# A fused attention and mixer block: x loads split and re-ordered around the query weights, two transposes moved from TensorE to DMA, a 384/128 last store, new instruction sequences

## The chip, the cores and the metric

One NeuronCore of a Trainium2 chip runs the whole program in one launch. The metric is device time in microseconds (us); lower is better. Five engines run their own instruction streams: TensorE (PE, matrix products into PSUM), VectorE (DVE), ScalarE (ACT), GpSimd (POOL) and SyncE (SP, here only a queue that issues DMAs). They wait for each other on semaphores alone.

## What is computed

x is 2048 tokens by 512 features, bfloat16. A pre-norm linear-attention block with 32 heads is followed by a pre-norm gMLP block whose spatial mixing multiplies a 2048 by 2048 matrix.

```python
def _A_ref(x, wqkv, wo):                       # x is layernorm(x)
    qkv = ...(x @ wqkv)...
    phi = lambda t: jnp.where(t > 0, t + 1, jnp.exp(t)) + 1e-06
    pq, pk = (phi(q), phi(k))
    kv = jnp.einsum('bhsd,bhse->bhde', pk, v)
    z = jnp.einsum('bhsd->bhd', pk)
    num = jnp.einsum('bhqd,bhde->bhqe', pq, kv)
    den = jnp.einsum('bhqd,bhd->bhq', pq, z)[..., None] + 1e-06
    return (num / den)... @ wo
def _B_ref(x, w_in, w_sp, b_sp, w_out):        # x is layernorm(h)
    z = _gelu(jnp.einsum('bsd,df->bsf', x, w_in))
    z1 = z[..., :Fh].copy()
    z2 = _layernorm(z[..., Fh:], axis=-1)
    g = jnp.einsum('ts,bsf->btf', w_sp, z2) + b_sp[None, :, None]
    return jnp.einsum('bsf,fd->bsd', z1 * g, w_out)
h = x + _A_ref(_layernorm(x, axis=-1), A_wqkv, A_wo)
return h + _B_ref(_layernorm(h, axis=-1), B_w_in, B_w_sp, B_b_sp, B_w_out)
```

## The kernel before

The 2048 tokens are 16 tiles of 128 (tile 0 to 15), in four groups of four. All weights and activations stay in SBUF.

**How order is made.** The program lists every operation once, with what it reads and writes. Two written-out tables then fix the execution: `ORDER` is a permutation of all operations, from which each engine takes its own in turn, and `SLOT` gives every PSUM or scratch tile its place. `schedule()` reads both, adds a wait wherever an operation needs what another engine wrote, or a PSUM bank that another still holds, and `run()` issues the waits and the instructions. The costs written into the operations play no part in execution. Each engine is strictly in order, so an instruction that waits holds all behind it. SP issues in this order: the loads of x and of the key and query weights, the DMA transposes of normalised x, 16 DMA transposes of the mixing matrix, those of the second block's input, the other 48 of the mixing matrix, the stores. POOL issues the loads of the value weights (wv), `w_in`, `wo`, the bias and `w_out`; wv waits for the last DMA transpose of normalised x, and `w_in` and `wo` stand behind it.

**The first stage**, where most of the change lies. For each tile n:

- DVE takes mean and variance (`stats`, L568, and the aggregate, L572). 1/sqrt is made on ACT for tiles 0 to 3 (Ln L582, Exp L584), and on POOL for the pairs from (4, 5) on (two steps, L587 and L589). DVE normalises (L603).
- The normalised tile is transposed. For tiles in `X_BY_PE` PE does it in four products of 128 columns (L633, "TR n" below), and ACT copies the result from PSUM (L640). For the others SP issues a DMA transpose (L625), which needs neither PE nor ACT.
- PE makes the keys of the tile, four products of 512 columns (L715, "K n"). For each pair of tiles ACT takes the exponential (L692) and for odd pairs the relu (L694), and DVE joins them to the feature map phi (L695, then L698 or, on even pairs, L701).
- PE multiplies the normalised tile with phi of the keys, summing over all tiles (L747, "XK n.0" and "XK n.1", two products each).
- For each group PE makes the queries of its four tiles in four blocks of 128 features (L729, "Q g f", four products each), which needs all four transposes of the group; phi on them runs as for keys.

Before the first transposes PE has nothing to multiply. It runs products of constants (L556, `keep_busy`, "idle products"): eight at once, three that wait for the first statistics, one that waits for the first Exp, and later two short ones of 256 columns after each of TR 0 and TR 1.

**The rest.** The sums over the keys (L759), den/spread steps (L829, L844), attention output (L879), second layernorm, the two halves of the first gMLP product (L911, L942), the spatial mixing (L981, 448 products), and the output product (L999), whose result DVE adds to h (L1005) and SP stores (L1007). The last tile's output is made in two passes of 256 columns.

Of the kernel before, what the change touches and what calls it, by code (L numbers as in the profile page):

```python
# [10 lines left out]
P = 128  # L11
# [1 line left out]


ORDER = [
# [36 lines left out]
]  # L52
SLOT = [
# [6 lines left out]
]  # L60


# [292 lines left out]
def bass_sequential_preLN__linear_attn_block__mixer_gmlp__prompt_kernel(  # L355
# [20 lines left out]
    WARM = 8  # L376
    EPS_PHI, EPS_DEN, EPS_LN = 1e-6, 1e-6, 1e-5
    CG = 32
    X_BY_PE, H_BY_PE = (0, 1, 2, 3, 4, 5), ()
    Q_RELU = (True, True, True, True)  # L380
    K_RELU = (1, 3, 5, 7)
    CENTRED = ()
    A_STATS = ()
    R_POOL = (4, 6, 8, 10, 12, 14)
    COPY_DVE = ()
    LN1 = [[0], [1], [2], [3], [4, 5], [6, 7], [8, 9], [10, 11], [12, 13], [14, 15]]
    N2_ACT = range(16)
    VIA_ACT = ((0, 0), (1, 0), (2, 0), (3, 0))
# [37 lines left out]
    def small(shape, dtype):  # L426
        n = (int(np.prod(shape)) * mybir.dt.size(dtype) + GRAIN - 1) // GRAIN * GRAIN
        o = at[0]
        at[0] += n
        return View(s_sm, o, shape, dtype)  # L430
# [60 lines left out]
    def load(eng, name, dst, src, nbytes, bias=0.0, behind=(), cost=0.5):  # L491
        o = op(eng, cost, lambda e: e.dma_start(dst.ap(), src), w=[dst], dma=(name, False), nbytes=nbytes,  # L492
               bias=bias, land=2.3)
        for p in behind:
            o.deps[p] = True
        return o
# [3 lines left out]
    BIG = 1000.0  # L500

    def load_x(eng, a, b, bias=BIG, **kw):
        more = {2: 103e3, 4: 70e3}.get(a, 0)
        xl[a] = load(eng, f"x{a}", x[a:b, :], x_dram[a * P:b * P, :].rearrange("(n p) d -> p n d", p=P),
                     int((b - a) * P * D * 2 + more), bias, **kw)

    load_x("sp", 0, 1)
    load_x("sp", 1, 2)
    load_x("sp", 2, 4)
    load("sp", "wk", wqkv[:, D:2 * D], w3[:, :, D:2 * D], D * D * 2 + 50000)  # L510
    for a in (4, 6):
        load_x("sp", a, a + 2)
    for a in (8, 10):
        load_x("sp", a, a + 2)
    load_x("sp", 12, 16)
    load("sp", "wq", wqkv[:, 0:D], w3[:, :, 0:D], D * D * 2)
    for a, b in zip(g.ops, g.ops[1:]):
        b.after.append(a)

# [89 lines left out]
    def normalise_act(dst, src, rs, nm, n=512):  # L609
        op("act", act_c(n, 2) + 0.04, lambda e: e.activation(dst.ap(), src.ap(), ACT.Identity, bias=nm.ap(), scale=rs.ap()),  # L610
           r=[src, rs, nm], w=[dst])

    def minus(m, rs, nm):
        op("pool", 0.25, lambda e: e.tensor_scalar(nm.ap(), m.ap(), -1.0, None, op0=ALU.mult), r=[m], w=[nm])
        op("pool", 0.25, lambda e: e.tensor_tensor(nm.ap(), nm.ap(), rs.ap(), ALU.mult), r=[nm, rs], w=[nm])
# [31 lines left out]
    for grp in LN1:  # L647
# [21 lines left out]
        rs_op[grp[0]] = g.ops[-1]  # L669
        for i, n in enumerate(grp):  # L670
            d = xn1[n, :]
            normalise(d, x[n, :], Row(st_x, n), 6, rs[i:i + 1], negative=n in A_STATS)
            transposed(n, lambda d=d: d, xT, n in X_BY_PE)

    for gate, n, cost, count in ((first[0], 512, 2 * MM, 3), (rs_op[0], 512, 2 * MM, 1), (tr_op[0], 256, MM, 2),
                                 (tr_op[1], 256, MM / 2, 2)):
        for i in range(count):
            keep_busy(n, cost, [], [gate] if gate.eng != "pe" else [])
            if gate.eng == "pe":
                g.ops[-1].after.append(gate)  # L680
# [335 lines left out]
                for n in range((tg - 1) * TPG, tg * TPG):  # L1016
                    project(n, [(0, D)])
    for n in range((NG - 1) * TPG, NT):
        project(n, [(0, D)] if n < NT - 1 else [(0, D // 2), (D // 2, D)])


    g.schedule()
# [55 lines left out]
```

## Time and profile before

| | us |
|---|---|
| median of 3 runs (243.77 to 244.08) | 244.07 |
| the profiled execution's own time | 243.96 |
| its span, first to last instruction | 242.2 |

The profile is of that one execution. "Busy" is time in which an engine has an instruction in flight. Products on PE overlap, so a row of several products is read by the distance from its start to the next row's start. A row of the timeline gives its start, its length, engine and line, the operation, its output and input, how many instructions it merges, and, in brackets, idle time before it and what ended that. SPq and POOLq are the queues on which DMAs are issued; the time "to landing" runs from the issue to the completion.

### The profile page before, as it was taken

What the parts mean: (1) busy time and instruction counts of PE and PEld (TensorE: products, weight loads), DVE (VectorE), ACT (ScalarE), POOL (GpSimd) and SP (SyncE); (2) the same over time, 40 slices, a digit from 0 to 9 for tenths busy, and PEclk for the clock granted to TensorE, in tenths of its full rate; (3) what the DMA queues carried; (4) which work ended last, traced back from release to release, by engine and by line L of the source; (5) the groups of instructions that cost most, each with busy time, mean ns of one, the idle gap of its engine ahead of it and who ended that gap; (6) DMA issues with size and microseconds to landing.
All of it is one profiled execution on the core that took longest, in us unless ns stands there. A gap on an engine that the chain in (4) does not pass through costs nothing.

```text
span 242.2 us, 3026 instructions
## 1 busy us (share of the span) xinstructions
PE 238.3 (98%) x1175; PEld 108.8 (45%) x1175; DVE 135.2 (56%) x269; ACT 85.1 (35%) x107; POOL 34.1 (14%) x87
## 2 busy tenths in 40 slices
PE   8999999999999999999999999999999999999995
PEld 3544443433444444445444444444444444444443
DVE  4999654589999967656533223251332513322443
ACT  3875744898588598564500010000000000000000
POOL 5316021002316542122100000000000000000000
DMA  6920459954324231459344444446200100000022
GB/s 199 321 43 18 94 106 337 232 122 96 46 43 128 47 46 22 87 119 231 88 108 92 107 86 95 100 108 94 83 0 0 65 24 0 0 0 3 0 87 87
DMA packets 55598, 21.57 MB, mean 89 GB/s; under 512 B 49472, under 2 KB 54720, under 8 KB 55584
## 3 DMA queue, kind: packets, MB, share of 16 engines
q1 hardware_dynamic: 54640, 17.05, 32.7%
q0 software_dynamic: 944, 4.33, 5.5%
q8 instruction: 9, 0.15, 0.3%
q14 instruction: 5, 0.04, 0.1%
HBM read 7.47 MB, written 2.10 MB: 40 GB/s over the span
## 4 chain that ended last, share of the span: by engine, by line
PE 91%; DVE 4%; DMA 2%; ACT 2%; SPq 1%; issue 0%
PE ps L981 40%; PE ps L942 10%; PE ps L911 10%; PE ps L999 10%; PE ps L747 6%; PE ps L879 5%; PE ps L715 5%; PE ps L729 4%; DMA xh<-in_A_x_dram 2%; DVE small L568 1%; SPq L492 1%; DVE xT_pq_z L698 1%; DVE xh L884 0%; DVE xT_pq_z L859 0%; DVE e L695 0%; PE ps L844 0%
## 5 line engine op out<-in xcount | busy, mean ns | idle before, releaser
L981 PE MATMUL ps<-wsp,pk_xn_z 128*128 128x512 bf16 x336 | 73.8, 379 | 0.0
L988 DVE TENSOR_TENSOR e<-ps,e 128x512 bf16<-128x512 f32 x28 | 19.4, 691 | 66.0 <-PE ps L981 66.0
L981 PEld LDWEIGHTS ps<-wsp,pk_xn_z 128*128 128x128 bf16 x336 | 32.8, 98 | 39.5
L942 PE MATMUL ps<-hT,win 128*128 128x512 bf16 x112 | 26.6, 379 | 0.0
L911 PE MATMUL ps<-win,hT 128*128 128x512 bf16 (+1 forms) x128 | 26.0, 353 | 0.0
L999 PE MATMUL ps<-wout,xT_pq_z 128*128 128x512 bf16 (+1 forms) x119 | 24.7, 367 | 0.0
L981 PE MATMUL ps<-wqkv_wsp,pk_xn_z 128*128 128x512 bf16 x112 | 24.3, 379 | 0.0
L947 ACT ACTIVATE xT_pq_z<-ps 128x1024 bf16<-128x1024 f32 (+1 forms) x16 | 14.4, 913 | 23.9 <-PE ps L942 23.9
L568 DVE BATCH_NORM_STATS2 small<-xh 128x6 f32<-128x512 bf16 x32 | 20.7, 678 | 3.3 <-DMA xh<-in_A_x_dram 3.3
L920 DVE BATCH_NORM_STATS2 small<-pk_xn_z 128x6 f32<-128x512 bf16 (+1 forms) x32 | 18.3, 611 | 7.2 <-ACT pk_xn_z L916 7.1
L692 ACT ACTIVATE e<-ps 128x1024 bf16<-128x1024 f32 x16 | 16.5, 1029 | 9.7 <-PE ps L715 6.1
L911 PEld LDWEIGHTS ps<-win,hT 128*128 128x128 bf16 x128 | 12.5, 98 | 12.7 <-ACT e L854 0.3
L916 ACT ACTIVATE pk_xn_z<-ps 128x896 bf16<-128x896 f32 x16 | 14.5, 914 | 8.9 <-PE ps L911 8.8
L1005 DVE TENSOR_TENSOR e<-ps,xh 128x512 bf16<-128x512 f32 (+1 forms) x17 | 11.2, 660 | 11.3 <-PE ps L999 11.3
L999 PEld LDWEIGHTS ps<-wout,xT_pq_z 128*128 128x128 bf16 x119 | 11.6, 98 | 12.8
L981 PEld LDWEIGHTS ps<-wqkv_wsp,pk_xn_z 128*128 128x128 bf16 x112 | 11.0, 98 | 13.2
L942 PEld LDWEIGHTS ps<-hT,win 128*128 128x128 bf16 x112 | 10.9, 98 | 12.6 <-ACT pk_xn_z L916 0.4
L589 POOL TENSOR_TENSOR small<-small 128x2 f32<-128x2 f32 x22 | 16.0, 727 | 1.2
L587 POOL TENSOR_SCALAR small<-small 128x2 f32<-128x2 f32 x22 | 6.4, 297 | 67.6 <-DVE small L572 67.4
L747 PE MATMUL ps<-pk_xn_z 128*128 128x512 bf16 x64 | 15.6, 379 | 0.0
L729 PE MATMUL ps<-xT_pq_z,wqkv_wsp 128*128 128x512 bf16 x64 | 15.5, 380 | 0.0
L715 PE MATMUL ps<-wqkv_wsp,xT_pq_z 128*128 128x512 bf16 x64 | 15.3, 379 | 0.0
(72 smaller groups left out, 191.0 us busy)
## 6 DMA issues: line engine op xcount, KB each, us to landing
out_dram<-e SPq DMA_DIRECT2D x15, 128.0 KB, 1.7
win<-in_B_w_in_dram POOLq DMA_DIRECT2D x1, 1792.0 KB, 9.2
xh<-in_A_x_dram SPq DMA_DIRECT2D x5, 256.0 KB, 4.7
wqkv_wsp<-in_A_wqkv_dram SPq DMA_DIRECT2D x2, 512.0 KB, 5.7
wout<-in_B_w_out_dram POOLq DMA_DIRECT2D x1, 896.0 KB, 6.4
wsp<-in_B_w_sp_dram SPq DMA_TRANSPOSE x48, 2.9
xh<-in_A_x_dram SPq DMA_DIRECT2D x1, 512.0 KB, 6.2
wqkv_wsp<-in_A_wqkv_dram POOLq DMA_DIRECT2D x1, 512.0 KB, 4.8
```

What stands on the lines that cost most here:

```text
L568: op("dve", dve_c(512), lambda e: e.bn_stats(s6.ap(), src.ap()), r=[src], w=[s6])
L589: return op("pool", 0.7, lambda e: e.tensor_tensor(dst.ap(), dst.ap(), h.ap(), ALU.pow), r=[dst, h], w=[dst])
L692: op("act", act_c(n), lambda e: e.activation(lo.ap(), t(flat).ap(), ACT.Exp), r=[t()], w=[lo])
L715: i = e.matmul(t(bank(ti)).ap(), lhsT=lhs.ap()[:, c, :], rhs=rhs.ap()[:, c, :], start=(c == 0), stop=(c == KD - 1))
L729: r_ = e.matmul(t(bank(i)).ap(), lhsT=lhs.ap()[:, c, :], rhs=rhs.ap()[:, c, :], start=(c == 0), stop=(c == KD - 1))
L747: r = e.matmul(txk[h](bank(i)).ap(), lhsT=xx.ap()[:, c * P:(c + 1) * P], rhs=kk.ap(), start=(n == 0), stop=(n == NT - 1))
L911: k = e.matmul(t(bank(i)).ap()[:, 0:b - a], lhsT=l.ap()[:, c, :], rhs=win[c, a:b].ap(), start=(c == 0), stop=(c == KD - 1))
L920: op("dve", dve_c(b - a), lambda e, s6=s6, src=src: e.bn_stats(s6.ap(), src.ap()), r=[src], w=[s6])
L942: k = e.matmul(t(bank(i)).ap(), lhsT=l.ap()[:, c, :], rhs=r_.ap()[:, c, :], start=(c == 0), stop=(c == KD - 1))
L981: k = e.matmul(t(bank(0)).ap(), lhsT=l.ap()[:, s - a, :], rhs=r_.ap()[:, s - a, :], start=(s == 0), stop=(s == NT - 1))
L988: op("dve", dve_c(512), lambda e: e.tensor_tensor(gb().ap(), t(bank(0)).ap(), bsp().ap()[:, tg * GW:(tg + 1) * GW], ALU.add), r=[t(), bsp( ...
L999: k = e.matmul(t(bank(0)).ap()[:, 0:b - a], lhsT=l.ap()[:, fc, :], rhs=wout[fc, a:b].ap(), start=(fc == 0), stop=(fc == KF - 1))
```

## The change

Parts:

1. The x load of tiles 2 and 3 together becomes two loads, of tile 2 ahead of the key weights and of tile 3 behind them. The load of the query weights moves from the end of SP's list to ahead of the load of tiles 4 and 5.
2. Tiles 4 and 5 are no longer transposed by PE but by DMA: eight products and two ACT copies are gone, two DMA transposes are added at the head of SP's ten.
3. Of the three idle products that wait for the first statistics one is dropped.
4. The last tile's output is made in passes of 384 and 128 columns in place of 256 and 256.
5. `ORDER` and `SLOT` are new throughout (nearly every number differs; their lines are left out below).

Two helpers that nothing uses are added as well (`normalise_pool`, and lists `N1_POOL`, `N1_ACT` that are empty). The byte figures in `load_x` (`more`) enter the planned costs alone.

```diff
-    X_BY_PE, H_BY_PE = (0, 1, 2, 3, 4, 5), ()
+    X_BY_PE, H_BY_PE = (0, 1, 2, 3), ()
...
+    N1_POOL = ()
+    N1_ACT = ()
...
     load_x("sp", 0, 1)
     load_x("sp", 1, 2)
-    load_x("sp", 2, 4)
+    load_x("sp", 2, 3)
     load("sp", "wk", wqkv[:, D:2 * D], w3[:, :, D:2 * D], D * D * 2 + 50000)
+    load_x("sp", 3, 4)
+    load("sp", "wq", wqkv[:, 0:D], w3[:, :, 0:D], D * D * 2)
     for a in (4, 6):
         load_x("sp", a, a + 2)
     for a in (8, 10):
         load_x("sp", a, a + 2)
     load_x("sp", 12, 16)
-    load("sp", "wq", wqkv[:, 0:D], w3[:, :, 0:D], D * D * 2)
...
-    for gate, n, cost, count in ((first[0], 512, 2 * MM, 3), (rs_op[0], 512, 2 * MM, 1), (tr_op[0], 256, MM, 2),
+    for gate, n, cost, count in ((first[0], 512, 2 * MM, 2), (rs_op[0], 512, 2 * MM, 1), (tr_op[0], 256, MM, 2),
                                  (tr_op[1], 256, MM / 2, 2)):
...
-        project(n, [(0, D)] if n < NT - 1 else [(0, D // 2), (D // 2, D)])
+        project(n, [(0, D)] if n < NT - 1 else [(0, D - P), (D - P, D)])
```

Read out of the two `ORDER` tables, the instructions of PE from the end of the first idle products on, up to XK 8.0:

```
before: TR 0, idle, idle, TR 1, idle, idle, K 0, TR 2, K 1, K 2, TR 3, TR 4, TR 5, K 3, K 4, Q g0 f0, Q g0 f1,
  K 5, XK 0.0, 0.1, 1.1, 1.0, Q g0 f2, Q g0 f3, XK 2.0, 3.0, 2.1, 3.1, K 6, K 7, XK 4.1, 5.1, Q g1 f2, Q g1 f3,
  XK 4.0, 5.0, Q g1 f0, Q g1 f1, XK 6.0, K 8, K 9, XK 6.1, K 10, XK 7.1, K 11, XK 7.0, XK 8.0
after:  TR 0, idle, TR 1, idle, TR 2, idle, idle, K 0, K 2, TR 3, K 1, Q g0 f2, K 3, Q g0 f0, Q g0 f3, Q g0 f1,
  XK 0.1, 1.1, 0.0, 1.0, K 4, K 5, XK 2.0, 3.0, 2.1, 3.1, K 6, K 7, XK 4.0, Q g1 f0, Q g1 f1, XK 5.0, K 8,
  XK 4.1, K 9, Q g1 f2, Q g1 f3, XK 5.1, 6.1, 7.1, 6.0, 7.0, XK 8.0
```

and those of DVE in the new order, from the first tile to the phi of keys 8 and 9 ("join" is L701 or L698):

```
stats 0, 1, aggr 0, 1, stats 2, aggr 2, norm 0, 1, 2, stats 3, aggr 3, norm 3, stats 4, 5, aggr 4, 5, stats 7, 6,
min k0, norm 4, aggr 7, norm 5, join k0, aggr 6, stats 8, min k1, stats 9, norm 6, join k1, norm 7, stats 11,
aggr 9, 8, stats 10, min q0.0, stats 14, norm 8, min k2, aggr 14, join k2, aggr 10, norm 9, min q0.2, aggr 11,
stats 12, 15, join q0.2, aggr 15, norm 10, min k3, aggr 12, norm 11, stats 13, norm 15, aggr 13, join q0.0,
min q1.0, join k3, join q1.0, min k4, norm 12, join k4
```

ACT begins with Ln and Exp of tiles 0, 1 and 2 in both orders; then it copied TR 0 and TR 1 and took Ln 3, Exp 3, copy 2 and the first exponential (of keys 0 and 1), and now it copies TR 0, 1 and 2, takes Ln 3 and Exp 3, copies TR 3, and goes on to that exponential. POOL's order for the pairs is (4, 5), (6, 7), (8, 9), (10, 11), (14, 15), (12, 13), and that of SP's transposes follows the tiles' numbers. Behind the sums over the keys, PE ran two den steps, Q g3 f0, the product with the value weights (L796), a spread step, Q g3 f1 and then the product with wo (L814); now two more blocks of queries and a second spread step stand ahead of L814: den, den, Q g2 f2, L796, spread, Q g2 f3, Q g2 f0, spread, Q g2 f1, L814.

More of the change, by code (lines that the diff above doesn't have):

```diff
@@ L502, in load_x @@
     def load_x(eng, a, b, bias=BIG, **kw):
-        more = {2: 103e3, 4: 70e3}.get(a, 0)
+        more = {2: 40e3, 3: 60e3, 4: 70e3}.get(a, 0)
         xl[a] = load(eng, f"x{a}", x[a:b, :], x_dram[a * P:b * P, :].rearrange("(n p) d -> p n d", p=P),
@@ L611, in normalise_act, with normalise_pool @@
            r=[src, rs, nm], w=[dst])
+    def normalise_pool(dst, src, m, rs):
+        op("pool", 0.9, lambda e: e.tensor_scalar(dst.ap(), src.ap(), m.ap(), rs.ap(), op0=ALU.subtract,
+                                                  op1=ALU.mult), r=[src, m, rs], w=[dst])
     def minus(m, rs, nm):
@@ L671, in bass_sequential_preLN__linear_attn_block__mixer_gmlp__prompt_kernel @@
             d = xn1[n, :]
-            normalise(d, x[n, :], Row(st_x, n), 6, rs[i:i + 1], negative=n in A_STATS)
+            if n in N1_POOL:
+                normalise_pool(d, x[n, :], st_x[n, 6:7], rs[i:i + 1])
+            elif n in N1_ACT:
+                nm = small([1], FP32)
+                minus(st_x[n, 6:7], rs[i:i + 1], nm.all())
+                normalise_act(d, x[n, :], rs[i:i + 1], nm.all())
+            else:
+                normalise(d, x[n, :], Row(st_x, n), 6, rs[i:i + 1], negative=n in A_STATS)
             transposed(n, lambda d=d: d, xT, n in X_BY_PE)
-    for gate, n, cost, count in ((first[0], 512, 2 * MM, 3), (rs_op[0], 512, 2 * MM, 1), (tr_op[0], 256, MM, 2),
+    for gate, n, cost, count in ((first[0], 512, 2 * MM, 2), (rs_op[0], 512, 2 * MM, 1), (tr_op[0], 256, MM, 2),
                                  (tr_op[1], 256, MM / 2, 2)):
```

84 rows, old and new, of tables (ORDER, SLOT) are left out of this document.

## The prediction

> **What bounds the kernel now.** I read the chain of waits first, then busy time by stretches, then the timelines of the first 12 us.
>
> ```profile
> PE 91%; DVE 4%; DMA 2%; ACT 2%; SPq 1%; issue 0%
> ```
> ```profile
> 0.00:6.00 6.00, 5.17 (x14) 1.78 (x15) 2.85 (x9) 2.22 (x6) 3.60 (x22) 1.00 0.67 197
> 6.00:11.00 5.00, 4.59 (x39) 2.52 (x38) 4.83 (x16) 3.96 (x9) 1.00 (x2) 1.00 1.09 354
> 12.00:24.00 12.00, 12.00 (x57) 5.49 (x56) 12.00 (x30) 8.27 (x10) 4.95 (x9) 1.00 0.13 27
> 48.00:80.00 32.00, 31.85 (x162) 13.87 (x161) 31.28 (x54) 25.79 (x33) 8.40 (x21) 1.00 0.40 86
> 80.00:230.00 150.00, 150.00 (x708) 69.10 (x707) 65.31 (x133) 28.89 (x34) 12.67 (x29) 1.00 0.30 64
> ```
>
> The columns are the stretch, its length, and busy time of PE, PEld, DVE, ACT and POOL; the granted clock, DMA share and GB/s end the row. PE is the bound from 12 us to the tail, with no hole worth the name. So time can be won in two ways: fewer products, or real products that begin earlier. DVE is just as full from 12 to 24 and nearly so from 48 to 80; it is second in line. What PE does at the start:
>
> ```profile
> 0.83 5.25 PE L556 MATMUL ps<-const-bfloat16-1.0 128*128 128x512 bf16 x12 [0.83 <-PEq L1063]
> 5.91 0.40 PE L633 MATMUL ps<-small,pk_xn_z 128*128 128x128 bf16 x4
> ...
> 7.00 1.04 PE L715 MATMUL ps<-wqkv_wsp,xT_pq_z 128*128 128x512 bf16 x4
> 7.87 0.39 PE L633 MATMUL ps<-small,pk_xn_z 128*128 128x128 bf16 x4
> 8.09 1.89 PE L715 MATMUL ps<-wqkv_wsp,xT_pq_z 128*128 128x512 bf16 x8
> 9.82 0.39 PE L633 MATMUL ps<-small,pk_xn_z 128*128 128x128 bf16 x4
> 10.59 0.72 PE L633 MATMUL ps<-small,pk_xn_z 128*128 128x128 bf16 x8 [0.38 <-DVE pk_xn_z L603]
> 11.14 1.89 PE L715 MATMUL ps<-wqkv_wsp,xT_pq_z 128*128 128x512 bf16 x8
> ```
>
> From row to row, a transposed tile costs 0.22 (7.87 to 8.09), a key block K 0.865 (8.09 to 9.82 is two). TR 3 begins at 9.82 and TR 4 only at 10.59: PE stands 0.55 there and waits for the normalised tile 4. K 3 begins at 11.14, and from there PE never stops until the sums over the keys. Why tile 4 is late:
>
> ```profile
> 2.68 4.51 DMA xh<-in_A_x_dram
> ```
>
> In the chain, the load of tiles 4 and 5 takes from 2.68 to 7.19, and PE reaches for them as soon as DVE has them.
>
> **The change, part by part.** I compare the moment when PE begins K 3 with the whole remainder (K 3 to K 15, all Q, all XK) before it. Before, that is 11.14, with all transposes done.
>
> DVE, ACT and POOL of the same stretch:
>
> ```profile
> 2.98 1.29 DVE L568 BATCH_NORM_STATS2 small<-xh 128x6 f32<-128x512 bf16 x2 [2.98 <-DMA xh<-in_A_x_dram]
> ...
> 5.26 0.40 DVE L603 TENSOR_SCALAR pk_xn_z<-xh,small 128x512 bf16<-128x512 bf16 x1
> ```
> ```profile
> 4.83 0.33 ACT L584 ACTIVATE small<-small 128x1 f32<-128x1 f32 x2
> 5.78 0.29 ACT L582 ACTIVATE small<-small 128x1 f32<-128x1 f32 x1 [0.62 <-DVE small L572]
> 6.11 0.20 ACT L584 ACTIVATE small<-small 128x1 f32<-128x1 f32 x1
> 6.34 1.08 ACT L640 ACTIVATE xT_pq_z<-ps 128x512 bf16<-128x512 bf16 x2
> ```
> ```profile
> 8.81 0.29 POOL L587 TENSOR_SCALAR small<-small 128x2 f32<-128x2 f32 x1 [4.57 <-DVE small L572]
> 9.19 0.71 POOL L589 TENSOR_TENSOR small<-small 128x2 f32<-128x2 f32 x1
> ```
>
> *x tile 2 alone, one idle product less.* Exp of tile 0 is done near 5.02 (4.83 and half of the pair), but its normalise starts at 5.26, behind the statistics of tile 2, which had to wait for 256 KB. With 128 KB I put them before 4.5, so norm 0 runs 5.1 to 5.5 and norm 1 to 5.8. Ln and Exp of tile 2 begin at 5.2 in place of 5.78 and end near 5.75; norm 2 ends at 6.2. PE's eleven products end one (5.08/12 = 0.42) earlier than 5.91, at 5.48: TR 0 at 5.65, TR 1 at 5.95, TR 2 at 6.3. ACT's first copy no longer waits for Exp 2 (its end at 6.31 is where the copies began): it starts 0.2 after TR 0, near 6.05, and ends at 6.65. K 0 begins at 6.7, with three transposes done where before it was 7.00 with two. If tile 2 does not land sooner than the pair did, K 0 stays at 7.0: those are the two ends, 0 and 0.3; I take 0.3, as the row of the load of two tiles leaves no reason for a half load to take as long.
>
> *K 0 to K 3.* Copies follow each other at 0.5: copy 2 ends at 7.65, so K 2, now ahead of K 1, waits 0.13 and runs 7.7 to 8.56. Tile 3 lands behind the key weights; its Ln waits for ACT until 7.55, Exp ends at 8.05, norm 3 at 8.5, so TR 3 fits at 8.57, then K 1 from 8.8 to 9.65. K 3 follows, one query block having been drawn ahead of it. PE thus has the same remainder before it at 9.65, against 11.14: **1.49 earlier**. By parts: 0.3 (start), 0.22 (TR 2 already in), 0.45 (TR 4, TR 5 gone), 0.6 (their wait gone, with its restart), less 0.13 and some hundredths.
>
> *Tiles 4 and 5 by DMA, query weights first.* The 512 KB put ahead of them take 1.48 at the 354 GB/s of the row from 6 to 11: landing at 8.67 in place of 7.19. Statistics 8.7 to 9.95, aggregates to 10.2, POOL's two steps 1.1 (8.81 to 9.90) to 11.4, norm 4 ends at 12.05, norm 5 at 12.45.
>
> ```profile
> xT_pq_z<-pk_xn_z SPq DMA_TRANSPOSE x10, 2.5
> ```
> ```profile
> 22.62 10.35 SPq L625 DMA_TRANSPOSE xT_pq_z<-pk_xn_z  x8
> ```
>
> A DMA transpose lands after 2.5 and holds SP 1.3 (10.35/8): tile 4 at 14.6, tile 5 at 15.9. PE wants K 4 after five blocks and four half blocks from 9.65, at 15.7, and K 5 at 16.55. Covered by 1.1 and 0.65; without that cover each 0.1 of lateness is 0.1 of time.
>
> *The new order up to K 15.* All later tiles now come from a DVE that starts their statistics at 8.7. Its costs:
>
> ```profile
> L568 DVE BATCH_NORM_STATS2 small<-xh 128x6 f32<-128x512 bf16 x11 | 7.2, 679 | 0.0
> L603 DVE TENSOR_SCALAR pk_xn_z<-xh,small 128x512 bf16<-128x512 bf16 x13 | 5.0, 402 | 0.0
> L695 DVE TENSOR_SCALAR e<-e 128x1024 bf16<-128x1024 bf16 x9 | 3.7, 416 | 2.2 <-ACT e L694 2.1
> L698 DVE TENSOR_TENSOR xT_pq_z<-e 128x1024 bf16<-128x1024 bf16 x4 | 2.8, 689 | 0.1
> L701 DVE SCALAR_TENSOR_TENSOR pk_xn_z<-ps,e 128x1024 bf16<-128x1024 f32 x2 | 2.4, 1207 | 0.0
> L572 DVE BATCH_NORM_AGGREGATE small<-small 128x2 f32<-128x6 f32 x12 | 1.9, 171 | 0.0
> ```
>
> Each overlaps the next by 0.08 (the pair at 2.98 takes 1.29, not 1.38), so the steps are 0.60, 0.32, 0.34, 0.61, 1.13 and 0.09. From stats 4 to the join of keys 4 and 5 there are 9, 5, 4, 1, 2 and 7 of them: 11.9, done at 20.7. PE wants it for XK 4.0 after nine blocks and eight half blocks (0.432) from 9.65: 20.9. To the join of keys 8 and 9 come another 3, 5, 4, 4, 1 and 5: 8.8, done at 29.5; PE wants it at 29.5 (six blocks, eight halves more). So PE and DVE run neck and neck, and the transposes of tiles 6 to 11 land one to three us before their K. What this costs is 0 if x lands as early as its bandwidth allows (8.3, were it not held up before 6 us), up to 0.4 with a landing at 9: I take 0, nearer to the middle of these.
>
> *Last store.*
>
> ```profile
> 239.00 0.42 DVE L1005 TENSOR_TENSOR e<-ps,xh 128x256 bf16<-128x256 f32 x1
> 239.76 0.42 DVE L1005 TENSOR_TENSOR e<-ps,xh 128x256 bf16<-128x256 f32 x1 [0.34 <-PE ps L999]
> ```
> ```profile
> 240.21 0.33 SPq L1007 DMA_DIRECT2D out_dram<-e  x1
> ```
>
> A pass of 256 columns takes 0.76 of PE. With 384 first, the first add starts 0.38 later, 239.38, and takes 0.55 (between 0.42 and the 0.69 that a stats row shows for 512 columns); its store is issued from 239.95 to 240.28. The small add ends at 240.12, but its store waits for SP: 240.32 against 240.21. So this part loses 0.1, or nothing if the smaller store lands that much sooner. I take 0.1.
>
> Sum against the profiled execution: 243.96 - 1.49 + 0.10 = **242.6**. The median of the runs shown is 244.07, 0.1 above it; I leave the number. Its own range is 242.1 (another few tenths, as the new order also moves the few short waits of 48 to 80) to 243.0.
>
> **Rivals.** *A: DVE falls behind.* Of the two that run neck and neck, DVE sets the pace from 9 to 30 us; it has no hole in the row from 12 to 24, and now starts 1.5 later on tile 4. Against it: it stood idle from 26 us on in the old order (2.2 in the L695 row). At a landing of 9.2 and half a us of slower POOL steps, PE loses 0.4 to 0.9: 243.0 to 243.5, say 243.2.
>
> *B: given back at L814.*
>
> ```profile
> 36.30 0.75 POOL L492 DMA_DIRECT2D wqkv_wsp<-in_A_wo_dram  x1
> ```
> ```profile
> wqkv_wsp<-in_A_wo_dram POOLq DMA_DIRECT2D x1, 512.0 KB, 10.2
> ```
> ```profile
> 47.98 1.03 PE L814 MATMUL ps<-wqkv_wsp,wsp 128*128 128x512 bf16 x4
> ```
>
> The weight loads wait for the last transpose of x, and wo lands at 46.5, 1.5 ahead of its use. In the new order norm 13 and 14 end near 30, so tile 15's transpose goes out at 32.4, 0.7 later than the 31.7 that the eight from 22.62 give, and wo lands at 47.2. PE reaches L814 near 48.7 (two blocks and a spread further on, 1.4 earlier). Should wo land at 50.1, because DVE's norms slip by 2.9, all is lost: 244.0, no change.
>
> *C: slower, the clock.* The twelve idle products take 0.42 each, every later one of that size 0.216; the row to 6 us grants 1.00 all the same, so that column doesn't show it. PE worked 5.1 without a hole before it doubled its rate. Eleven products leave a hole, from 5.48 to 5.65. If that starts the count again, PE runs at half rate to 10.7: TR 0 takes 0.2 more, and of the 4.0 from 6.7 on half is lost: 242.6 + 2.2 = **244.8**. It decides at any pause before the rate doubles. Against it: the hole is short, and the transposes are products too. [...]
>
> **How the numbers follow.** The forecast has 0.60, A 0.18, B (no change, from whatever later wait) 0.10, C and its like (the new order stalling PE further on) 0.12. About 0.2% (0.5 us) can be told from no change. Forecast and A are faster: 0.78; same 0.10; slower 0.12. The range takes the forecast's low end, 242.0, and reaches over A to near B, 243.9.
>
> **What would show it.** K 0 near 6.7, K 1's end near 9.65, no idle time ahead of L633; tiles 4 and 5 landing near 8.7 and their transposes out near 12.1; the sums over the keys, L759, some 1.5 earlier than now. A wait of PE for DVE's L701 near 21 or 29.5 would be A; for the load of wo near 49, B; products of 0.43 behind 5.9, C. The last two stores issued back to back would confirm the loss at the end. The forecast is wrong if L759 comes that much earlier and the gain is gone by 80 us.

## The result, and the profile after

The changed kernel takes 242.94 us (median of 19 runs, 242.60 to 245.87) against 244.11 for the kernel before on the same chip (19 runs, 243.77 to 245.76): a ratio of 0.9962, with a 95% interval of 0.9944 to 0.9980. Its profiled execution took 242.84, with a span of 241.1.

The page's fourth part, the chain of waits, is of PE alone now; the shares of DVE and of the load of x are gone.

```profile
PE 98%; issue 1%; DVEq 0%; DVE 0%
```

Busy time by stretches, changed kernel (columns as before: stretch, length, PE, PEld, DVE, ACT, POOL; then clock, DMA share, GB/s):

```profile
0.00:6.00 6.00, 5.13 (x13) 1.58 (x14) 2.94 (x8) 2.49 (x7) 3.61 (x22) 1.00 0.64 177
6.00:11.00 5.00, 5.00 (x37) 2.62 (x36) 3.82 (x11) 3.37 (x7) 0.42 (x2) 1.00 1.10 358
12.00:24.00 12.00, 11.95 (x56) 5.42 (x56) 12.00 (x32) 8.85 (x10) 3.27 (x7) 1.00 0.34 68
```

From 6 to 11 PE is full: the holes of 0.41 in sum are closed. From 12 to 24 DVE is still full to the last hundredth. The timeline of PE to 12 us, changed kernel:

```profile
0.83 5.00 PE L559 MATMUL ps<-const-bfloat16-1.0 128*128 128x512 bf16 x11 [0.83 <-PEq L1077]
5.87 0.49 PE L640 MATMUL ps<-small,pk_xn_z 128*128 128x128 bf16 x4
...
7.08 1.98 PE L729 MATMUL ps<-wqkv_wsp,xT_pq_z 128*128 128x512 bf16 x8
8.90 0.39 PE L640 MATMUL ps<-small,pk_xn_z 128*128 128x128 bf16 x4
9.12 1.03 PE L729 MATMUL ps<-wqkv_wsp,xT_pq_z 128*128 128x512 bf16 x4
9.99 1.03 PE L743 MATMUL ps<-xT_pq_z,wqkv_wsp 128*128 128x512 bf16 x4
```

K 1 ends at 9.99 (Q g0 f2 begins), where the prediction had 9.65. The 0.3 that the start was to win is missing: K 0 begins at 7.08. DVE's rows, same execution, say why:

```profile
3.72 0.69 DVE L571 BATCH_NORM_STATS2 small<-xh 128x6 f32<-128x512 bf16 x1 [0.18 <-DMA xh<-in_A_x_dram]
...
5.34 1.09 DVE L606 TENSOR_SCALAR pk_xn_z<-xh,small 128x512 bf16<-128x512 bf16 x3
6.64 0.69 DVE L571 BATCH_NORM_STATS2 small<-xh 128x6 f32<-128x512 bf16 x1 [0.20 <-DMA xh<-in_A_x_dram]
...
8.90 1.29 DVE L571 BATCH_NORM_STATS2 small<-xh 128x6 f32<-128x512 bf16 x2
```

DVE had to wait for tile 1 until 3.72 (before, the statistics of tiles 0 and 1 ran in one piece from 2.98), so the normalise steps start at 5.34 and not at 5.1. Tiles 4 and 5 are there by 8.90.

Positions in PE's order, by the first weight load of each in the traces (us; "again" is a second profile of the changed kernel as it is, "halves" an experiment below):

| | before | after | again | halves |
|---|---|---|---|---|
| K 0 | 6.99 | 7.05 | 6.65 | 6.73 |
| K 1 | 8.04 | 9.07 | 8.76 | 8.86 |
| XK 8.0 | 32.70 | 29.63 | 30.77 | 29.42 |
| sums over the keys | 41.45 | 40.31 | 41.23 | 40.08 |
| first output product of the last group | 227.24 | 225.96 | 226.89 | 225.73 |
| last tile's output product | 237.82 | 236.53 | 237.46 | 236.30 |
| last store landed | 241.75 | 240.63 | 241.56 | 240.44 |

In the profiled execution, against before: 1.15 earlier where the remainder begins (K 3 at 11.14 before, the end of K 1 at 9.99 now), 1.14 at the sums, 1.28 at the output products, 1.12 at the last landing. The gain is made before 10 us, is kept, and some 0.15 of it is lost behind the last product.

### The profile page after: what moved, and what is told of

Same layout as the page of the kernel before. It is cut to its first block, busy times and chain, and to the rows that moved or that the text cites. A ratio compares the mean times of both kernels' runs of the same rounds, so it can differ in the third digit from the quotient of the medians.

```text
span 241.1 us, 2991 instructions
## 1 busy us (share of the span) xinstructions
PE 236.2 (98%) x1143; PEld 107.6 (45%) x1166; DVE 135.3 (56%) x269; ACT 84.3 (35%) x105; POOL 33.9 (14%) x87
## 4 chain that ended last, share of the span: by engine, by line
PE 98%; issue 1%; DVEq 0%; DVE 0%
PE ps L995 40%; PE ps L925 10%; PE ps L956 10%; PE ps L1013 10%; PE ps L893 6%; PE ps L743 6%; PE ps L729 6%; PE ps L761 6%; PE ps L559 2%; PE ps L858 1%; PE ps L843 1%; PE ps L640 0%; PE ps L773 0%; PE ps L828 0%; PE ps L810 0%
## 5 line engine op out<-in xcount | busy, mean ns | idle before, releaser
L925 PE MATMUL ps<-win,hT 128*128 128x384 bf16 (+1 forms) x124 | 26.0, 352 | 0.2
L1013 PE MATMUL ps<-wout,xT_pq_z 128*128 128x512 bf16 (+2 forms) x117 | 24.6, 366 | 0.1
L925 PEld LDWEIGHTS ps<-win,hT 128*128 128x128 bf16 x128 | 12.4, 98 | 12.6 <-issue 0.2
L1019 DVE TENSOR_TENSOR e<-ps,xh 128x512 bf16<-128x512 f32 (+2 forms) x17 | 11.1, 659 | 11.4 <-PE ps L1013 11.4
L956 PEld LDWEIGHTS ps<-hT,win 128*128 128x128 bf16 x112 | 11.0, 98 | 12.6
L761 PE MATMUL ps<-pk_xn_z 128*128 128x512 bf16 x63 | 15.2, 379 | 0.2 <-issue 0.2
```

Source lines behind the costliest of these rows:

```text
L761: r = e.matmul(txk[h](bank(i)).ap(), lhsT=xx.ap()[:, c * P:(c + 1) * P], rhs=kk.ap(), start=(n == 0), stop=(n == NT - 1))
L925: k = e.matmul(t(bank(i)).ap()[:, 0:b - a], lhsT=l.ap()[:, c, :], rhs=win[c, a:b].ap(), start=(c == 0), stop=(c == KD - 1))
L956: k = e.matmul(t(bank(i)).ap(), lhsT=l.ap()[:, c, :], rhs=r_.ap()[:, c, :], start=(c == 0), stop=(c == KD - 1))
L1013: k = e.matmul(t(bank(0)).ap()[:, 0:b - a], lhsT=l.ap()[:, fc, :], rhs=wout[fc, a:b].ap(), start=(fc == 0), stop=(fc == KF - 1))
```

## The experiments

The theory: the gain is the head's (transposes and their wait gone), and whether it is kept is decided by whether DVE gets tiles 4 and 5 in time. The rivals: a single part brings it, or the gain hangs on another margin (queries, wo, the tail). Where only one number of a run is given, it is the median. Each ratio is to the kernel before, run beside it on the same chip.

**256/256 store in the changed kernel** (`e1_store256`).

```diff
-        project(n, [(0, D)] if n < NT - 1 else [(0, D - P), (D - P, D)])
+        project(n, [(0, D)] if n < NT - 1 else [(0, D // 2), (D // 2, D)])
```

> The changed kernel with the last tile's output in passes of 256 and 256 columns again. My theory, that 384/128 loses 0.1 us because the small store waits on SP for the large one: 0.11 us faster than the changed kernel (242.94), 242.83; the two last stores are issued 0.76 apart, the last one 0.45 after the one before it has left SP. The rival, that the split of the last tile changes nothing: 242.94, and the last landing stands as far behind the start of OUT 8 as in the changed kernel (14.7 us).

242.85, ratio 0.9941 (0.9920 to 0.9961): no difference to the changed kernel that the intervals could show. From the last tile's output product to the last landing it took 4.15, against 4.10 in the changed kernel and 3.93 in the kernel before. So it is no undoing. The weight loads and DVE's adds of this run show the reason:

```profile
237.68 0.66 PEld L1011 LDWEIGHTS ps<-wout,xT_pq_z 128*128 128x128 bf16 x7 [0.30 <-DVE e L1017]
238.66 0.42 DVE L1017 TENSOR_TENSOR e<-ps,xh 128x256 bf16<-128x256 f32 x1 [0.54 <-PE ps L1011]
```

The second pass waits 0.30 for DVE's add of tile 14: the new `SLOT` gives it PSUM bank 7, which tile 14's output holds (the kernel before gave it a bank that had been free for long). With 384 columns first the wait disappears behind the longer first pass: in the profile after, twelve weight loads run from 236.91 to 238.26 without one. The run with its own bank, below, does without that wait.

**Third idle product back** (`e2_idle3`): the count of the first entry of the loop of idle products is 3 in place of 2.

> The changed kernel with the third idle product put back. My theory: in its profile TR 0 (5.87) waits for norm 0 of tile 0 (done at 5.72), not for PE, and a twelfth product would end at 5.91, so the dropped product is worth 0.0 to 0.05 us: 242.95. The rival, which my forecast held in part (products end 0.42 earlier and TR 0 with them): K 0 starts 0.2 to 0.3 later, 243.2. A second rival, the clock: with an unbroken start the rate doubles earlier, and time falls by some tenths.

242.83, ratio 0.9936 (0.9916 to 0.9957). PE's rows of this run:

```profile
0.83 5.28 PE L558 MATMUL ps<-const-bfloat16-1.0 128*128 128x512 bf16 x12 [0.83 <-PEq L1076]
...
7.25 1.98 PE L728 MATMUL ps<-wqkv_wsp,xT_pq_z 128*128 128x512 bf16 x8
9.32 0.40 PE L639 MATMUL ps<-small,pk_xn_z 128*128 128x128 bf16 x4
```

K 0 comes at 7.25, and the median is none the worse. TR 3 is why: here tile 3 landed at 7.32 and TR 3 came 2.00 later (statistics, Ln, Exp, normalise). K 0 and K 2 take 1.73, so an earlier K 0 only waits for tile 3. This profiled execution took 243.25, 0.41 more than the one after, and it is behind by as much at the sums over the keys already (40.73 against 40.31), as tile 3 landed 0.7 later. The clock rival is out: with the unbroken start the rate of PE doubled near 6.4, not earlier than in the profile after (near 6.1).

**Tiles 2 and 3 in one load again** (`e3_pair`), ahead of the key weights.

```diff
-    load_x("sp", 2, 3)
+    load_x("sp", 2, 4)
...
-    load_x("sp", 3, 4)
```

> The changed kernel with x tiles 2 and 3 in one load again, ahead of the key weights. My theory after the profile: statistics of tile 2 start at 4.65 in place of 4.55, norm 0 comes 0.1 later, K 0 at 7.15 to 7.2, and tile 3 being early buys nothing: 0.1 us slower than the changed kernel, 243.05. The forecast's reading (the half load is worth the whole 0.3 of the start): 243.25. The rival that the split is worth nothing, since K 0 is set by the landing of tile 1: 242.94.

243.10, ratio 0.9955 (0.9937 to 0.9972); the profiled execution took 243.69. The statistics of tile 2 had to wait for the pair until 4.86, norm 0 began at 5.69 (5.34 in the profile after), and K 1 came at 9.44, 0.37 later; and its tiles 4 and 5 landed at 10.12. PE's row then:

```profile
15.05 1.90 PE L758 MATMUL ps<-pk_xn_z 128*128 128x512 bf16 x8 [0.21 <-DVE pk_xn_z L712]
```

So the split is worth some 0.35 at the start of that profile, more than the 0.1 expected. What of it reaches the end is not shown: the late tiles 4 and 5 cost time there too, and the ratio cannot be told from the changed kernel's 0.9962.

**The DMA transposes alone** (`e4_dma_only`), in the kernel before with its own order and its own loads.

```diff
-    X_BY_PE, H_BY_PE = (0, 1, 2, 3, 4, 5), ()
+    X_BY_PE, H_BY_PE = (0, 1, 2, 3), ()
```

> The kernel before with one thing changed: tiles 4 and 5 transposed by DMA, loads and order as before. My theory, that the move pays only because the query weights come early and let PE make queries while the transposes are under way: K 3 starts near 10.9, K 4 has to wait for tile 4's transpose (norm 4 at 10.55, landing 13.1), so the query blocks begin 1.1 later than before: 245.2, slower than before by 0.4%. The rival, that eight products and their wait off PE are worth 1.0 wherever they are taken out: 243.1.

245.27, slower: ratio 1.0043 (1.0010 to 1.0076). PE:

```profile
10.71 1.04 PE L713 MATMUL ps<-wqkv_wsp,xT_pq_z 128*128 128x512 bf16 x4 [0.69 <-ACT xT_pq_z L638]
13.04 1.04 PE L713 MATMUL ps<-wqkv_wsp,xT_pq_z 128*128 128x512 bf16 x4 [1.30 <-DMA xT_pq_z<-pk_xn_z]
```

Eight products fewer, and PE stands first 0.69 for the copy of TR 3, which TR 4 and TR 5 used to cover, and then 1.30 for the DMA transpose of tile 4. The part saves PE's time only where other work stands ahead of K 4, and that work is query blocks, for which the query weights have to be there.

**The changed kernel once more** (`c_after`).

> The changed kernel unchanged, for its spread on the chip of the following three. My theory: TR 3 and with it K 1 come 2.0 us after tile 3 lands (6.6 to 7.3 in the profiles so far), and the landings of the first loads differ from execution to execution; so its times spread more than those of the kernel before, upwards by some tenths: median 242.9, from 242.6 to 244.

243.17 (242.44 to 244.77, 11 runs), ratio 0.9957 (0.9937 to 0.9978); the profiled execution took 243.76, 0.92 more than the first one. The chain of waits:

```profile
PE 93%; DMA 3%; DVE 2%; SPq 1%; issue 0%; DVEq 0%
```

PE's timeline, same execution:

```profile
5.58 0.38 PE L640 MATMUL ps<-small,pk_xn_z 128*128 128x128 bf16 x4 [0.26 <-DVE pk_xn_z L606]
...
6.68 1.98 PE L729 MATMUL ps<-wqkv_wsp,xT_pq_z 128*128 128x512 bf16 x8
8.58 0.40 PE L640 MATMUL ps<-small,pk_xn_z 128*128 128x128 bf16 x4
8.81 1.03 PE L729 MATMUL ps<-wqkv_wsp,xT_pq_z 128*128 128x512 bf16 x4
9.67 1.03 PE L743 MATMUL ps<-xT_pq_z,wqkv_wsp 128*128 128x512 bf16 x4
...
15.08 1.90 PE L761 MATMUL ps<-pk_xn_z 128*128 128x512 bf16 x8 [0.93 <-DVE pk_xn_z L715]
```

and DVE's:

```profile
10.18 1.29 DVE L571 BATCH_NORM_STATS2 small<-xh 128x6 f32<-128x512 bf16 x2 [1.66 <-DMA xh<-in_A_x_dram]
...
13.81 1.22 DVE L715 SCALAR_TENSOR_TENSOR pk_xn_z<-ps,e 128x1024 bf16<-128x1024 f32 x1
```

Here the start came off as forecast, and more than it won was lost behind it: the query weights landed at 9.41 instead of 8.12 and tiles 4 and 5 at 10.16 instead of 8.88, with the same list of loads. DVE, strictly in order, stands for 1.66 ahead of the statistics of tile 4 with the join of keys 0 and 1 queued behind them, and PE waits 0.93 for that join. Median and spread came out somewhat above the expected (242.9, up to 244).

**256 KB more ahead of tiles 4 and 5** (`e6_delay_x4`): tiles 0 and 1 loaded once more, behind the query weights, to a place that nothing reads.

```diff
     load("sp", "wq", wqkv[:, 0:D], w3[:, :, 0:D], D * D * 2)
+    load("sp", "xd", xc[0:2, :], x_dram[0:2 * P, :].rearrange("(n p) d -> p n d", p=P), 2 * P * D * 2)
```

> The changed kernel with 256 KB more to load (two tiles of x into memory that is free then) between the query weights and x tile 4, so that tile 4 lands 0.75 later, near 9.6. Rival A of the prediction as theory (DVE and PE run neck and neck; DVE has some 0.25 us in hand): PE waits at K 4, XK 4.0 or XK 8.0 for 0.5 in all: 243.4, 0.5 slower than the changed kernel. The other theory, that the covers of the forecast (1.1 and 0.65 at the transposes) take it up: no change, 242.9.

243.36 as expected, ratio 0.9964 (0.9948 to 0.9980). In the profiled execution (243.75) tiles 4 and 5 landed at 10.14 (9.6 expected), and from the sums over the keys on it runs with the late profile of the changed kernel (41.23 both); PE's row:

```profile
15.07 1.90 PE L761 MATMUL ps<-pk_xn_z 128*128 128x512 bf16 x8 [0.86 <-DVE pk_xn_z L715]
```

So a late landing of tiles 4 and 5, and of the tiles behind them in the list, brought about by the load put ahead, gives the slow profile. The wait is not at K 4, XK 4.0 or XK 8.0, as expected, but at the first XK, for the join of keys 0 and 1.

**Query weights in halves around tiles 4 and 5** (`e7_halves`), with the 256/256 store: features 256 to 511 first, which the first query block needs.

```diff
-    load("sp", "wq", wqkv[:, 0:D], w3[:, :, 0:D], D * D * 2)
-    for a in (4, 6):
-        load_x("sp", a, a + 2)
-    for a in (8, 10):
+    H = D // 2
+    load("sp", "wqa", wqkv[:, H:D], w3[:, :, H:D], D * D)
+    load_x("sp", 4, 6)
+    load("sp", "wqb", wqkv[:, 0:H], w3[:, :, 0:H], D * D)
+    for a in (6, 8, 10):
```

> The changed kernel with passes of 256 and 256 columns at the end, and with the query weights loaded in two halves, features 256 to 511 ahead of x tile 4 and the rest behind it. Tile 4 lands 0.75 earlier, near 8.1; the query blocks of the first half are made first and the others from 11.5 on. Theory A: PE is not faster in a good execution, since there it never waited for DVE, but one with late loads is: 0.1 from the store, and a smaller spread than the changed kernel, median 242.75. The rival, that DVE holds PE in most executions: 0.3 or more faster, 242.5 or less.

242.80 (242.64 to 242.98, 6 runs), ratio 0.9939 (0.9924 to 0.9954). Tiles 4 and 5 landed at 8.40; the profiled execution, 242.64, is 1.37 ahead of the kernel before at the sums over the keys and 1.51 at the output products. The median is the expected one. The smaller spread (0.34) is not shown to be the halves' doing: the run with its own bank, below, has the same list of loads and spreads over 0.86.

**Also tile 3 ahead of the key weights** (`e8_early`), with an order of the first steps to fit: K 1 ahead of TR 3, statistics of tile 3 earlier.

> As the kernel with the weights in halves, and x tile 3 also ahead of the key weights, with the first instructions of DVE, ACT and PE in the order in which the tiles land (aggregate, Ln and Exp of a tile at once, K 0, K 1, K 2 in order). My theory, that the start is set by the wait of TR 3 on tile 3 and by K 0's place behind three transposes: K 0 follows the landing of the key weights, near 6.55, K 2 ends near 9.6 in place of K 1 at 9.97, and DVE starts tile 4 near 8.3 in place of 8.9, so that nothing of the 0.4 is lost later: 242.4. The rival, that DVE's chain is the bound after all: 242.75, as with the halves alone. A third: PE stalls at its clock's first rate, 0.43 a product, for part of K 0 and K 1: 243 or more.

A miss: 243.40, ratio 0.9964 (0.9949 to 0.9980). In the profiled execution, a good one at 243.00, K 0 started at 7.06, just behind the key weights, which landed at 6.92 in place of some 6.3. That the weights lost what tile 3 won is argued, not shown: with tile 3 behind them they landed anywhere from 6.06 to 7.40 in the other profiles.

**Own bank for the last pass** (`e9_bank`): the run of the halves, with entry 205 of `SLOT`, the PSUM bank of tile 15's second pass, 2 in place of 7.

> Query weights in halves around x tiles 4, 5, last store in passes of 256 and 256, and the second pass put into another PSUM bank (2 in place of 7, which tile 14's output still holds). Theory: with 256/256 in the new order the second pass waited for the add of tile 14 (0.30 in the run of the halves), so undoing the 384/128 store could not show its price. With a bank of its own the stretch from the last tile's first weight load to the last landing is 3.93, as in the kernel before, against 4.10 with 384/128 and 4.15 with 256/256 and the shared bank: 242.6. Rival: the end is set by the stores alone, the stretch stays 4.1 and the time 242.8.

243.07 (242.50 to 243.36; 242.6 expected), ratio 0.9954 (0.9937 to 0.9971). From the last tile's output product to the last landing: 3.93, as expected. The add of the second pass, this run:

```profile
238.70 0.42 DVE L1019 TENSOR_TENSOR e<-ps,xh 128x256 bf16<-128x256 f32 x1 [0.34 <-PE ps L1013]
```

and in the changed kernel:

```profile
238.08 0.76 DVE L1019 TENSOR_TENSOR e<-ps,xh 128x384 bf16<-128x384 f32 x2 [0.45 <-PE ps L1013]
```

The median does not show the 0.2: tiles 4 and 5 landed at 9.22 in the profiled execution, which took 242.90. It is 0.46 behind the halves at the sums over the keys (40.54 against 40.08) and wins 0.21 of that back behind the last product.

**Whole query weights behind tiles 4 and 5** (`e10_x4_first`), with the same bank and 256/256.

> As the run before, but the whole query weights behind x tiles 4, 5. Theory: DVE's chain from the landing of tiles 4, 5 sets the pace, and the query weights, landing near 8.9, are wanted only at 9.7 by Q g0 f2: no wait of PE, a small spread, 242.6. When the list lands a us late, the query weights come at 10 and PE waits 0.3 there. Rival: the query weights had to go first; Q g0 f2 waits half a us or more in every execution: 243.1.

243.13 (242.45 to 243.70, 8 runs), ratio 0.9955 (0.9939 to 0.9971). A miss: neither 242.6 nor a small spread. PE did not wait for the queries, although their weights landed at 9.87 in the profile, and the tail took 3.95. But that execution (243.70), the slowest of the eight, has two other waits in PE's timeline:

```profile
9.08 0.40 PE L637 MATMUL ps<-small,pk_xn_z 128*128 128x128 bf16 x4 [0.35 <-DVE pk_xn_z L603]
50.16 1.02 PE L825 MATMUL ps<-wqkv_wsp,wsp 128*128 128x512 bf16 x4 [0.82 <-ACT e L865]
```

The first is TR 3 behind a tile 3 that landed at 7.08. The second is the product with wo. It is put down to ACT's copy, which ended at 50.07; but wo landed at 50.02, and in the profile after the same product started while that copy still ran (49.03, the copy from 48.86 to 49.89). So it is wo, in this run:

```profile
wqkv_wsp<-in_A_wo_dram POOLq DMA_DIRECT2D x1, 512.0 KB, 12.6
```

and in the changed kernel's profile:

```profile
wqkv_wsp<-in_A_wo_dram POOLq DMA_DIRECT2D x1, 512.0 KB, 9.6
```

**DVE relieved, tiles 4 and 5 late** (`e11_delay_dve`): the 256 KB more, with the statistics of tile 6 behind the join of keys 0 and 1, and those of tiles 14 and 15 behind the join of keys 8 and 9, with the normalise of tile 15 after that of 14.

> The changed kernel with 256 KB more ahead of x tiles 4, 5, and DVE's list relieved: the statistics of tile 6 behind the join of keys 0 and 1, those of tiles 14 and 15 (1.4 of DVE) behind the join of keys 8 and 9. Theory: with a late tile 4 it is DVE's list that PE waits for. The wait at L761 falls from 0.86 to under 0.4, XK 8.0 comes near 30.2 in place of 30.76, and the time is 243.1 against 243.36 (243.2 against 243.75 profile for profile). Rival: the DMA transposes of tiles 4, 5 set the pace (landing 6 after the tile, so 16.1 and 17.4): the wait only moves to K 4 and the time stays at 243.4 to 243.7.

A miss: 243.94, ratio 0.9994 (0.9978 to 1.0009), 0.6 above the run with the late tiles alone by the medians (the profiled executions, 243.82 and 243.75, hardly differ). Of the 0.86 at L761 some 0.3 is left, with tiles 4 and 5 landed at 9.83 in place of 10.14, but now the transposes by DMA are late:

```profile
20.86 1.04 PE L729 MATMUL ps<-wqkv_wsp,xT_pq_z 128*128 128x512 bf16 x4 [0.16 <-DMA xT_pq_z<-pk_xn_z]
```

Against the profile after, PE's products are 0.20 behind in K 6, 0.53 in K 7, 0.73 from XK 4.0 on, which waits for the join of keys 4 and 5, and 1.00 in K 13. That one starts at 34.29: tile 13's transpose landed at 34.25, in place of 32.20. DVE's list feeds the joins and the transposes alike, and moving these steps changed which of them was late.

**Query weights at the end of the list** (`e5_wq_last`).

> The changed kernel with the query weights at the end of SP's list again. Theory: they land near 12.4 and PE reaches Q g0 f2 near 9.8, so PE waits 2.6 there, and nothing later gives it back: 245.5. x tiles 4, 5 land near 7.2, which saves nothing as PE does not wait for DVE. Rival: the place of the query weights costs nothing, as the earlier tile 4 makes up for it: 242.9.

246.50, a single run. PE's row:

```profile
13.66 1.02 PE L741 MATMUL ps<-xT_pq_z,wqkv_wsp 128*128 128x512 bf16 x4 [2.62 <-DMA wqkv_wsp<-in_A_wqkv_dram]
```

The wait is the expected one; the other us is a late start of this execution (its key weights landed at 7.40, K 0 came at 7.50).

**What they say together.** The nine profiles that share the changed kernel's order up to the sums over the keys, in one table: the landing of tiles 4 and 5, the start of K 1, the landing less that start, and the stretch from K 1 to the sums (both by weight loads, good to about 0.1).

| | tiles 4, 5 | K 1 | difference | stretch |
|---|---|---|---|---|
| query weights behind 4, 5 | 7.72 | 9.26 | -1.54 | 31.23 |
| halves | 8.40 | 8.86 | -0.46 | 31.22 |
| after | 8.88 | 9.07 | -0.19 | 31.24 |
| third idle product | 9.55 | 9.50 | 0.05 | 31.22 |
| 256/256 store | 9.14 | 9.07 | 0.07 | 31.22 |
| own bank | 9.22 | 8.89 | 0.33 | 31.64 |
| pair 2, 3 | 10.12 | 9.44 | 0.68 | 31.76 |
| 256 KB more | 10.14 | 8.81 | 1.33 | 32.42 |
| changed, again | 10.16 | 8.76 | 1.40 | 32.47 |

In these profiles the stretch is 31.2 where the tiles landed no more than 0.1 behind the start of K 1, whatever else differs. Behind that each us of difference costs 0.8 to 1.3 us (0.54 over 0.68, 0.42 over 0.33). A head that starts earlier moves down in this table: it wins nothing if x does not come with it (from "after" to "changed, again" K 1 is 0.31 earlier and the stretch 1.23 longer).

No version is shown to beat the changed kernel: the halves have the best median and the third idle product the best ratio (0.9936), but both intervals overlap that of the change itself, and own bank and halves together came out at 243.07. Two parts were not taken out of the changed kernel by themselves: the transposes of tiles 4 and 5 (put back on PE) and the new order.

## Why the prediction was right, point by point

**The sum** was 242.6 for 242.84 profiled, with a median of 242.94. The mechanism held; terms were off in size. Against before, the profiled execution won 1.14 up to the sums and 0.14 more up to the output products and lost 0.16 behind them, where the forecast had 1.49 won and 0.10 lost. (Its list of parts adds up to 1.44; the 1.49 is the direct difference, 11.14 less 9.65.) That this execution was one with early loads is luck: the other profile of the kernel took 243.76, which lies beyond the forecast's own 243.0 and is covered only by rival A.

*x tile 2 alone, one idle product less* (0.3) is the step that failed in the execution it was made for: it gave nothing there. Tile 1 landed at 3.70 in place of 3.39, norm 0 began at 5.34 (5.05 in the second profile), and TR 0 came 0.29 later than there. Another 0.11 was lost as the four products of TR 0 still ran in part at PE's first, slow rate (0.33 to the next product, against 0.22). In the second profile of the same kernel the figures of that paragraph and the next are there: TR 0 at 5.58 (5.65 forecast), K 0 at 6.68 (6.7), TR 3 at 8.58 (8.57), K 1 at 8.81 (8.8), its end at 9.67 (9.65). Not all of the reasons are: TR 0 followed norm 0 in both profiles, not the end of the idle products, so the idle product left out gave next to nothing to these starts. What the prediction lacked is a floor under TR 3: in no profile of its order does it come sooner than 2.0 us after tile 3 has landed. In the first profile it came 2.29 after it, as Ln 3 stood behind ACT's three copies, which is what the prediction had. In the runs of the 256/256 store, of the third idle product and of the query weights behind tiles 4 and 5 it came exactly 2.0 after the landing, and K 0's start no longer mattered: with the 256/256 store K 0 began at 6.66 and K 1 at 9.12, as in the profile after with its K 0 at 7.08.

*K 0 to K 3.* The whole 1.49 was 1.15 in the first profile, where it lacks little more than the 0.3 of the start, and 1.47 in the second (11.14 to 9.67).

*Tiles 4 and 5 by DMA.* The transposes' row in SP's timeline of the profile after:

```profile
12.25 10.09 SPq L632 DMA_TRANSPOSE xT_pq_z<-pk_xn_z  x6
```

Out at 12.25 (12.1 forecast); they landed at 14.82 and 16.08 (14.6, 15.9), and K 4's first product began at 16.03 (15.7 forecast; the head was 0.34 behind its forecast), its weight load at 15.82. The cover of 1.1 was 1.2 by the product and 1.0 by the weight load. That this part loses without cover is shown by the kernel that has it alone.

*The new order up to K 15* was the neck-and-neck race, and it was one. DVE's rows of the profile after:

```profile
19.52 1.22 DVE L715 SCALAR_TENSOR_TENSOR pk_xn_z<-ps,e 128x1024 bf16<-128x1024 f32 x1
...
28.22 1.22 DVE L715 SCALAR_TENSOR_TENSOR pk_xn_z<-ps,e 128x1024 bf16<-128x1024 f32 x1
```

The joins end at 20.74 and 29.44 (20.7, 29.5 forecast), and PE's weight loads want them at 21.00 and 29.63: margins of 0.2 to 0.3. At the join of keys 0 and 1, which ends at 13.74, the margin was 0.35 (weight load at 14.09), and that is the place where the second profile waits. The prediction priced a landing at 9.0 with up to 0.4; the run with the tiles at 9.22 lost 0.42.

*Last store.* It loses 0.17, not 0.1 (4.10 against 3.93; the four profiles without the new store and without the shared bank have 3.92 to 3.95). The sign and the reason were right: the last two stores were issued back to back, at 238.67 and 239.04 with 0.33 for the first. The run of the 256/256 store could not show the price because of the bank.

*Beyond the head*, 0.14 more came between the sums and the output products; the prediction had a few tenths there in its own range.

**The rivals.** *A, DVE falls behind*, happens: in the same kernel, in some executions. Its place is the join of keys 0 and 1, ahead of the two that the prediction watched (keys 4 and 5, keys 8 and 9), and its trigger is a late landing, not slow POOL steps. It priced 243.2; the profiled case is 243.76. Of the 30 runs of the changed kernel, 10 lie over 243.4. That all of these are such cases is argued from the one that was profiled.

*B, given back at the product with wo*, did not happen in either profile of the changed kernel (wo landed at 46.44, wanted at 49.03). But in one execution with another order of loads it landed at 50.02 and PE waited 0.82, with an issue only 0.5 later: the risk lies in wo's own time to land, 9.4 to 12.6 us in these profiles, more than in DVE's norms.

*C, the clock*, is refuted. The second profile of the changed kernel does not decide it, although it has two holes of about 0.25 (ahead of the last idle product and of TR 0): its idle products start at 3.35, 3.77, 4.09 and 4.31, so the rate had doubled near 4.0, before the holes, and the last idle product is short already:

```profile
4.93 0.39 PE L559 MATMUL ps<-const-bfloat16-1.0 128*128 128x512 bf16 x1 [0.24 <-ACT small L587]
```

In the profile after the rate doubled near 6.1, behind two holes of about 0.2 (5.05 to 5.22 and 5.65 to 5.87), and K 0's products are 0.216 apart from 7.08 on; a count of 5.1 begun again would have kept them at 0.43. The run of tiles 2 and 3 in one load has the longest hole ahead of the doubling:

```profile
6.21 0.52 PE L637 MATMUL ps<-small,pk_xn_z 128*128 128x128 bf16 x4 [0.53 <-DVE pk_xn_z L603]
6.57 0.27 PE L556 MATMUL ps<-const-bfloat16-1.0 128*128 128x256 bf16 x1
6.68 0.39 PE L637 MATMUL ps<-small,pk_xn_z 128*128 128x128 bf16 x4
6.90 0.27 PE L556 MATMUL ps<-const-bfloat16-1.0 128*128 128x256 bf16 x1
```

TR 0 takes 0.36 there and TR 1, right behind, the full rate's 0.22. Over all fourteen profiles the rate doubled between 3.5 and 6.6 us, and with the same instructions at 4.0 and at 6.1. The earliest of these moments, in the run of the halves, came 2.7 us after the first product, against 5.1 in the kernel before. What sets the moment is not shown.

## What to carry to other kernels

When a change lets the first engine start earlier, ask which loads must come earlier with it: here the gain is whole only if tiles 4 and 5 land by the time that K 1 starts. Where two engines run neck and neck, one profile shows one side of the race; take a second of the same kernel before believing a tenth. To undo one part of a change under a new plan of buffers, look whether the old form fits that plan: here it met a shared PSUM bank and hid the price it was to show.

## What was not expected of the hardware

With the same list of loads, the query weights landed at 8.12, 8.38, 8.80 and 9.41 in four profiles, while the bytes per us were the same (358 and 353 GB/s from 6 to 11 in the two of the changed kernel). The trace has sixteen completion signals for each load. Those of the query weights come between 7.60 and 8.12 in the first profile; in the second, fifteen come by 8.01 and the last at 9.41, and in the run of tiles 2 and 3 in one load fifteen by 7.98 and the last at 9.37. So one part in sixteen is late, and it is late again in the loads behind (tiles 4 and 5 of the second profile: fifteen by 9.09, the last at 10.16). What holds that part up stays open. In the second profile one packet of 1 KB took 1.07 us from 6.19 on, with a median of 0.046; but the run of the two tiles in one load has no recorded packet above 0.3 us behind 6 us, and single packets of 0.5 to 1.0 us near 3.5 us are in profiles whose loads came early as well (1.05 in the run of the halves). The transfer of wo varied by more, 9.4 to 12.6 us.
